# Pooled attention and a gated MLP: key rows in the order (key, pair), the first batch pooled on TensorE, new orders

## The chip, the cores and the metric

The kernel runs on one core of a Trainium2 chip. The core has TensorE (PE, matrix multiply), VectorE (DVE), ScalarE (ACT), GpSimd (POOL) and SyncE (SP, which here issues every DMA). The metric is device time in microseconds (us), the median of the runs shown; less is better.

## The reference, cut to what matters

```python
# q, k, v: (8 batches, 8 heads, 576 rows, 64), float32
k_p = k.reshape(B, H, 72, 8, D).mean(axis=3)      # keys and values are averaged over groups of 8 rows
v_p = v.reshape(B, H, 72, 8, D).mean(axis=3)
attn = softmax(q @ k_p^T / sqrt(D))               # 576 x 72 for each head
x = concat_heads(attn @ v_p)                      # (B, 576, 512)
h = relu(x @ w_in)                                # w_in 512 x 1024
u, v = h[..., :512], h[..., 512:]
v_n = (v - mean(v)) / sqrt(var(v) + 1e-6)
gated = u * (w_spatial @ v_n + b_spatial)         # w_spatial 576 x 576, over the rows of a batch
out = gated @ w_out                               # w_out 512 x 512
```

The weights w_in and w_out come as 64-bit floats, which the kernel takes apart into 32-bit halves.

## The kernel before

All eight batches run through one core, one after the other but overlapped. To keep float32 accuracy on TensorE's reduced-precision float32 format, most operands are split into a high and a low part, and a product is made of three matmuls (high by high, low by high, high by low).

The work of a batch is written as stages, each a Python generator whose `yield`s cut it into steps:

- `K` (`att_keys`): four DMAs (L289) bring the first 64 pooled groups of the keys of all heads into two staging tiles `st`, each 128 rows by 2 by 512 numbers (8 raw rows of 64 side by side); a fifth DMA (L276, `load_rest`) brings the other 8 groups into `st_r`. Then the 8 raw rows are added up: by DVE in three halvings (`pool_sum`, L257 and L262), or, where the stage's name ends in `^`, by TensorE in eight matmuls with the identity into one accumulator (`pool_pe`, L268), from where ACT copies them. The results are `kp` and `kr`.
- `KT` (`att_keys_t`): three transposes on TensorE (L312, L313), then four copies (L320, L321) into `kp_bd`, which holds the two heads of a pair block by block.
- `V` (`att_values`): the same for values (two DMAs at L335, one at L276), without transposes; results `vp` and `vr_s`. `W` splits them into high and low parts.
- `Q0` to `Q4` load 128 query rows each (64 in the last, L377) and transpose them (L382). `S0` to `S4` are scores (L394, into the one PSUM buffer `s_ps`) and softmax, `T` transposes the probabilities (L459, L461), `A` multiplies by the values (L477 to L480) and yields `xT`.
- `v`, `u`, `s`, `o` are the four matrix products of the MLP (L527 and L542, L568, L587 to L589, L610). `s` is followed by a product on DVE (L592), a high part on ACT (L598) and a low part on POOL (L601), which `o` reads.
- `wv`, `wu`, `wo`, `ws`, `wb` load and prepare blocks of the weights once. The 64-bit blocks cost ACT, DVE and POOL instructions each (L177 to L192); the low half comes either from POOL (L202, L204) or, with `^`, from three matmuls on TensorE (L196 to L198) and a copy on ACT (L200).

A `~` or `^` after a stage's name chooses such a variant. The order of everything is written out in three tables: `FIRST` for batch 0, `STEP` for batches 1 to 6, `LAST` for batch 7. Each word in them is one step of a stage; `-` and `+` move it to the batch before or after, capitals belong to the next batch. Instructions stand on each engine in exactly the order of that table, and every engine works strictly in its order. SP's queue of DMAs is one of them. Staging tiles of K, V, `ws` and `wo` share three buffers (tag "kv"), so a load waits until the tile that had its buffer has been read.

Quoted in short, what sets the shape of a key load before:

```python
keys = k[b].rearrange("(r a e) (s j) d -> r e a s (j d)", r=2, e=2, j=POOL)
nc.sync.dma_start(out=sts[r][:, e, :], in_=keys[r, e, :, :KM, :])
```

In DRAM one such DMA walks 2 pairs (a), in each 64 groups (s), in each 512 numbers that lie together (2 KB); in SBUF it fills 128 rows.

Of the kernel before, what the change touches and what calls it, by code (L numbers as in the profile page):

```python
# [8 lines left out]
F32 = mybir.dt.float32  # L9
# [14 lines left out]


FIRST = (
# [16 lines left out]
)  # L43
STEP = (
# [8 lines left out]
)  # L53
LAST = (
# [7 lines left out]
)  # L62


# [5 lines left out]
def pooled_attention_gmlp(ctx: ExitStack, tc: tile.TileContext, q, k, v, w_in, w_sp, b_sp, w_out, out):  # L70
    nc = tc.nc
    B, H, S, D = q.shape
    P = 128
# [196 lines left out]
    def ps_pool():  # L270
        return ps_big()[:, :(NG + 1) * D].rearrange("p (g d) -> p g d", d=D)
# [6 lines left out]

    def att_keys(t, b, alt=""):

        keys = k[b].rearrange("(r a e) (s j) d -> r e a s (j d)", r=2, e=2, j=POOL)
        kp = pl.tile([P, 2, 2, D], F32, name="kp", tag="kp")
        kr = pl.tile([2 * RR, 1, 2, D], F32, name="kr", tag="kr")
        acc = ps_pool() if "^" in alt else None
        sts = []
        for r in range(2):
            sts.append(pl.tile([P, 2, POOL * D], F32, name="st", tag="kv", bufs=3))
            for e in range(2):
                nc.sync.dma_start(out=sts[r][:, e, :], in_=keys[r, e, :, :KM, :])  # L289
            yield  # L290
        st = load_rest(k[b, :, KM * POOL:, :].rearrange("h (s j) d -> h s (j d)", j=POOL))
        yield
        for r in range(2):
            if acc is None:
                pool_sum(sts[r], kp[:, r])
            else:
                pool_pe(sts[r], acc[:, 2 * r:2 * r + 2, :])
            yield
        if acc is None:
            pool_sum(st, kr, nc.gpsimd if alt else nc.vector)  # L300
        else:
            pool_pe(st, acc[:2 * RR, NG:, :])
            yield
            nc.scalar.copy(kp.rearrange("p r e d -> p (r e) d"), acc[:, :NG, :])
            nc.scalar.copy(kr, acc[:2 * RR, NG:, :].unsqueeze(2).broadcast_to([2 * RR, 1, 2, D]))
        t["k"] = kp, kr

    def att_keys_t(kp, kr, alt=""):

        kt = ps_tr()  # L310
        for r in range(2):
            nc.tensor.transpose(out=kt[:, r * P:(r + 1) * P], in_=kp[:, r, :, :], identity=ident)  # L312
        nc.tensor.transpose(out=kt[:, 2 * P:2 * P + 2 * RR], in_=kr[:, 0, :, :], identity=ident[:2 * RR, :2 * RR])  # L313
        yield
        main = kt[:, :2 * P].rearrange("p (g s) -> p g s", g=NG)
        rest = kt[:, 2 * P:2 * P + 2 * RR].rearrange("p (g e s) -> p g e s", g=NG, e=2)
        for e in range(2):
            es = slice(e * D, (e + 1) * D)
            copy = nc.vector.tensor_copy if alt else nc.scalar.copy
            copy(kp_bd[es, :, e * SP:e * SP + KM], main[es])  # L320
            copy(kp_bd[es, :, e * SP + KM:(e + 1) * SP], rest[es, :, e, :])  # L321
            if e == 0:
                yield

    def att_values(t, b, alt=""):

        eng = nc.gpsimd if alt else nc.vector
        rows = v[b].rearrange("(g e) (s j) d -> g (e s) (j d)", e=2, j=POOL)
        vp = pl.tile([P, NG, D], F32, name="vp", tag="vp")
        vq = pl.tile([2 * RR, 1, D], F32, name="vq", tag="vq")  # L330
        acc = ps_pool() if "^" in alt else None
        sts, g2 = [], [slice(2 * r, 2 * r + 2) for r in range(2)]
        for r in range(2):
            sts.append(pl.tile([P, 2, POOL * D], F32, name="st", tag="kv", bufs=3))
            nc.sync.dma_start(out=sts[r], in_=rows[g2[r], :P].rearrange("g p f -> p g f"))  # L335
            yield
        st = load_rest(rows[:, P:])
        yield
        for r in range(2):
            if acc is None:  # L340
                pool_sum(sts[r], vp[:, g2[r], :], eng)
            else:
                pool_pe(sts[r], acc[:, g2[r], :])
            yield
        if acc is None:
            pool_sum(st, vq, eng)
        else:
            pool_pe(st, acc[:2 * RR, NG:, :])
            yield
            nc.scalar.copy(vp, acc[:, :NG, :])  # L350
            nc.scalar.copy(vq, acc[:2 * RR, NG:, :])
            yield
        vr_s = pl.tile([RR, NG, D], F32, name="vr_s", tag="vr_s")
        for r in range(2):
            rs = slice(r * RR, (r + 1) * RR)
            nc.vector.tensor_tensor(vr_s[:, 2 * r:2 * r + 2, :], vq[rs].broadcast_to([RR, 2, D]),
                                    mask[rs].unsqueeze(2).broadcast_to([RR, 2, D]), op=ALU.mult)
        t["v"] = vp, vr_s

    def att_values_split(vp, vr_s):  # L360
        for e in range(2):
# [328 lines left out]
```

## Time and profile before

| What | Value |
|---|---|
| runs | 618.44, 617.6, 617.88 us; median 617.88 |
| the profiled execution | 617.54 us |
| its span, first to last instruction | 615.7 us |
| TensorE busy | 573.3 us (93%) |
| VectorE, ScalarE, GpSimd busy | 346.1, 301.5, 266.6 us |
| mean granted TensorE clock | 0.989 |
| bytes moved by DMA | 46.15 MB, mean 75 GB/s |

The page's chain of work that ended last is TensorE for 88% of the span, with 4% on DMA and 3% on SP's queue:

```profile
PE 88%; DMA 4%; SPq 3%; ACT 2%; DVE 2%; issue 0%; DVEq 0%; ACTq 0%
```

"Busy" counts an engine's own work; "idle before" is the wait ahead of an instruction, and the name behind the arrow what ended it. An idle time matters only where the engine's next work is what the end of the kernel hangs on. Line numbers are those of the kernel before; in the changed kernel L289 is L290 and L335 is L337.

### The profile page before, as it was taken

What the parts mean: (1) busy time and instruction counts of PE and PEld (TensorE: products, weight loads), DVE (VectorE), ACT (ScalarE), POOL (GpSimd) and SP (SyncE); (2) the same over time, 40 slices, a digit from 0 to 9 for tenths busy, and PEclk for the clock granted to TensorE, in tenths of its full rate; (3) what the DMA queues carried; (4) which work ended last, traced back from release to release, by engine and by line L of the source; (5) the groups of instructions that cost most, each with busy time, mean ns of one, the idle gap of its engine ahead of it and who ended that gap; (6) DMA issues with size and microseconds to landing.
All of it is one profiled execution on the core that took longest, in us unless ns stands there. A gap on an engine that the chain in (4) does not pass through costs nothing.

```text
span 615.7 us, 9982 instructions
## 1 busy us (share of the span) xinstructions
PE 573.3 (93%) x3557; PEld 513.8 (83%) x3557; DVE 346.1 (56%) x809; ACT 301.5 (49%) x937; POOL 266.6 (43%) x394
## 2 busy tenths in 40 slices
PE   1177889999999999999999999999999999999997
PEld 0165779987899888998999888998999988998995
DVE  1389768973794676336664576346663665253320
ACT  1079648673665364164635374254634474353321
POOL 1024566486345643344524652354525562240430
PEclk9988989999999999999999999999999999999999
DMA  1694324333242131302221121303220000101002
GB/s 69 201 242 127 121 72 121 92 110 117 87 110 71 47 91 52 103 26 85 71 94 52 52 86 52 108 22 111 62 93 3 1 33 19 36 2 51 18 1 85
DMA packets 56433, 46.15 MB, mean 75 GB/s; under 512 B 38848, under 2 KB 40896, under 8 KB 56384
## 3 DMA queue, kind: packets, MB, share of 16 engines
q1 hardware_dynamic: 56384, 45.52, 24.5%
q8 instruction: 28, 0.46, 0.3%
q14 instruction: 21, 0.17, 0.1%
HBM read 36.08 MB, written 9.44 MB: 74 GB/s over the span
## 4 chain that ended last, share of the span: by engine, by line
PE 88%; DMA 4%; SPq 3%; ACT 2%; DVE 2%; issue 0%; DVEq 0%; ACTq 0%
PE mm L568 17%; PE mm L587 17%; PE mm L610 16%; PE mm L527 14%; PE s_ps L394 6%; PE tp L459 3%; PE mm L542 2%; PE tp L382 2%; DMA st<-in_k 2%; SPq L289 2%; DMA st_r<-in_k 2%; PE tp L477 1%; PE mm L589 1%; PE mm L588 1%; PE tp L480 1%; PE tp L478 1%
## 5 line engine op out<-in xcount | busy, mean ns | idle before, releaser
L568 PE MATMUL mm<-xT,win_h 128*128 128x320 f32 (+1 forms) x512 | 106.1, 300 | 0.0
L428 POOL TENSOR_TENSOR pm<-e,rs 128x576 f32<-128x576 f32 (+1 forms) x40 | 47.0, 1174 | 93.1 <-DVE rs L425 87.5
L568 PEld LDWEIGHTS mm<-xT,win_h 128*128 128x128 f32 x512 | 83.9, 190 | 1.8
L601 POOL TENSOR_TENSOR gT<-g,gT 128x256 fp32r<-128x256 f32 x64 | 47.5, 749 | 81.8 <-ACT gT L598 81.7
L527 PE MATMUL mm<-win_h,xT 128*128 128x512 f32 x256 | 82.0, 401 | 0.0
L610 PE MATMUL mm<-wout_h,gT 128*128 128x512 f32 x256 | 81.2, 398 | 0.0
L587 PE MATMUL mm<-wT_h,vn_h 128*128 128x256 f32 (+1 forms) x256 | 76.3, 298 | 0.0
L568 PE MATMUL mm<-xT,win_l 128*128 128x256 f32 (+1 forms) x256 | 75.9, 297 | 0.0
L587 PE MATMUL mm<-wT_h,vn_l 128*128 128x256 f32 (+1 forms) x256 | 75.6, 295 | 0.0
L587 PE MATMUL mm<-wT_l,vn_h 128*128 128x256 f32 (+1 forms) x256 | 75.4, 295 | 0.0
L592 DVE TENSOR_TENSOR g<-mm,ru 128x320 f32<-128x320 f32 (+1 forms) x64 | 28.4, 453 | 80.1 <-PE mm L589 75.1
L536 POOL TENSOR_TENSOR vn_l<-vv,vn_h 128x512 fp32r<-128x512 f32 x32 | 41.7, 1320 | 52.5 <-ACT vn_h L534 52.5
L610 PEld LDWEIGHTS mm<-wout_h,gT 128*128 128x128 f32 x256 | 47.2, 189 | 9.9
L527 PEld LDWEIGHTS mm<-win_h,xT 128*128 128x128 f32 x256 | 46.7, 188 | 10.0
L394 PE MATMUL s_ps<-kp_bd,qT 128*128 128x144 f32 (+1 forms) x320 | 49.7, 301 | 4.2 <-ACT e L420 2.8
L149 ACT ACTIVATE xT<-tp 128x256 fp32r<-128x256 f32 (+1 forms) x64 | 25.0, 414 | 58.1 <-PE tp L480 57.8
L527 PE MATMUL mm<-win_l,xT 128*128 128x512 f32 x128 | 50.7, 396 | 0.0
L610 PE MATMUL mm<-wout_l,gT 128*128 128x512 f32 x128 | 50.7, 396 | 0.0
L568 PEld LDWEIGHTS mm<-xT,win_l 128*128 128x128 f32 x256 | 48.7, 190 | 0.0
L394 PEld LDWEIGHTS s_ps<-kp_bd,qT 128*128 128x128 f32 (+1 forms) x320 | 43.2, 188 | 6.5 <-ACT e L420 3.5
L587 PEld LDWEIGHTS mm<-wT_h,vn_h 128*128 128x128 f32 x256 | 48.2, 188 | 0.4 <-DVE g L592 0.2
L587 PEld LDWEIGHTS mm<-wT_h,vn_l 128*128 128x128 f32 x256 | 48.2, 188 | 0.0
(146 smaller groups left out, 1311.9 us busy)
## 6 DMA issues: line engine op xcount, KB each, us to landing
st<-in_k SPq DMA_DIRECT2D x32, 256.0 KB
qt<-in_q SPq DMA_DIRECT2D x32, 256.0 KB
st<-in_v SPq DMA_DIRECT2D x16, 512.0 KB
out<-ob SPq DMA_DIRECT2D x32, 256.0 KB
stw<-in_moe_w_in SPq DMA_DIRECT2D x8, 512.0 KB
st<-in_moe_w_out SPq DMA_DIRECT2D x4, 512.0 KB
st<-in_moe_w_spatial SPq DMA_DIRECT2D x4, 288.0 KB
st_r<-in_k SPq DMA_DIRECT2D x8, 128.0 KB
```

What stands on the lines that cost most here:

```text
L149: nc.scalar.activation(hi, src, AF.Copy)
L289: nc.sync.dma_start(out=sts[r][:, e, :], in_=keys[r, e, :, :KM, :])
L394: nc.tensor.matmul(s_ps[:m, g // 2, (g % 2) * 2 * SP:(g % 2 + 1) * 2 * SP], lhsT=qT[:, g, :m], rhs=kp_bd[:, g, :], start=True, stop=True,)
L428: nc.gpsimd.tensor_tensor(pm[:m], em, rs[:m].unsqueeze(2).broadcast_to([m, H, SP]), op=ALU.mult)
L459: nc.tensor.transpose(out=tpv[:, g, :], in_=pm[:, g, :P], identity=ident[:m, :m])
L527: nc.tensor.matmul(a, lhsT=xT[:, i, o + c * P:o + (c + 1) * P], rhs=w[:, i, DH:], start=(i == 0 and j == 0), stop=(i == NK - 1 and j == 2))
L536: nc.gpsimd.tensor_tensor(t["vn_l"][:, c, :], vv, f32(t["vn_h"][:, c, :]), op=ALU.subtract)
L568: nc.tensor.matmul(a, lhsT=w[:, i, d * P:(d + 1) * P], rhs=xT[:, i, o + ts.start:o + ts.stop], start=(i == 0 and j == 0), stop=(i == NK - ...
L587: nc.tensor.matmul(a, lhsT=x[:, c, ds], rhs=y[:, c, ts], start=(c == 0 and j == 0), stop=False)
L592: nc.vector.tensor_tensor(g, a, t["ru"][:, d, ts], op=ALU.mult)
L601: nc.gpsimd.tensor_tensor(dst[:, d, 1, at:at + m], g[:, o:o + m], f32(dst[:, d, 0, at:at + m]), op=ALU.subtract)
L610: nc.tensor.matmul(a, lhsT=src[:, i, x, at:at + m], rhs=w[:, i, :], start=(i == 0 and j == 0), stop=(i == ND - 1 and j == 2))
```

## The change

Three things are changed at once. The key loads walk DRAM as 64 groups, in each 2 pairs, so that a row of SBUF is (key, pair) instead of (pair, key); the copies into `kp_bd` undo that order. In `FIRST` the stages K and V of batch 0 carry `^` and are pooled on TensorE. All three tables are new; the weight blocks with a low half on TensorE are five (wv0, wv3, wv1, wu1, wu2) instead of seven (wv1, wv3, wv2, wv0, wu2, wu0, wo3). The results `t["k"]` and `t["v"]` are named before the steps that fill them, so that a table may place the next stage's step earlier.

```diff
 FIRST = (
-    "wv1~^ wv1 wv1 -K wv1 -K wv3~^ -K -Q0 -V -K -K wv1 -K -Q0 wv3 -Q0 wv3 wv2^ -KT wv1 -KT -Q1 -V -V -KT -S0~ "
+    "ws2 ws2 -K^ ws2 wv0^ -K ws2 -K wv0 -K wv0 -K wv2 -K wv2 -K wv0 wv2 -KT wv2 -Q0~ -KT -Q0 -Q1 wv2 -V^ -Q0 "
...
 LAST = (
...
-    "s03 s00 s00 s11 s13 s02 s10 s12 s01 s01 s00 s03 s10 s03 s11 -o0 s12 s00 s02 s12 s12 s11 o1 o1 s11 o4 o2 "
-    "o3 o4 o2 o1 o3 o4 o0 o2 o3 o0 o0 "
+    "s01 s10 s03 s10 s11 s02 s11 s01 s10 s10 o0 o1 o1 -o3 s13 o1 s11 s13 s11 s13 s12 s13 o3 o3 o4 o3 o0 o0 o4 "
+    "o4 o2 o2 o2 "
...
     def att_keys(t, b, alt=""):
-        keys = k[b].rearrange("(r a e) (s j) d -> r e a s (j d)", r=2, e=2, j=POOL)
+        keys = k[b].rearrange("(r a e) (s j) d -> r e s a (j d)", r=2, e=2, j=POOL)
         kp = pl.tile([P, 2, 2, D], F32, name="kp", tag="kp")
         kr = pl.tile([2 * RR, 1, 2, D], F32, name="kr", tag="kr")
+        t["k"] = kp, kr
...
-                nc.sync.dma_start(out=sts[r][:, e, :], in_=keys[r, e, :, :KM, :])
+                nc.sync.dma_start(out=sts[r][:, e, :], in_=keys[r, e, :KM, :, :])
...
     def att_keys_t(kp, kr, alt=""):
-        main = kt[:, :2 * P].rearrange("p (g s) -> p g s", g=NG)
+        main = kt[:, :2 * P].rearrange("p (r s a) -> p r a s", r=2, a=2)
...
-            copy(kp_bd[es, :, e * SP:e * SP + KM], main[es])
+            copy(kp_bd[es, :, e * SP:e * SP + KM].rearrange("p (r a) s -> p r a s", r=2), main[es])
...
     def att_values(t, b, alt=""):
+        vr_s = pl.tile([RR, NG, D], F32, name="vr_s", tag="vr_s")
+        t["v"] = vp, vr_s
...
-        vr_s = pl.tile([RR, NG, D], F32, name="vr_s", tag="vr_s")
...
-        t["v"] = vp, vr_s
```

What this does to the engines' orders at the start. SP's queue of DMAs before, from its first (`stw` is a staged 64-bit weight block, `qt` a block of queries):

```order
L165 DMA stw<-in_moe_w_in 128x1024
L289 DMA st<-in_k 128x1x512 x4
L165 DMA stw<-in_moe_w_in 128x1024
L276 DMA st_r<-in_k 64x1x512
L377 DMA qt<-in_q 128x8x64
L335 DMA st<-in_v 128x2x512
```

and in the changed kernel:

```order
L237 DMA st<-in_moe_w_spatial 128x576
L290 DMA st<-in_k 128x1x512 x2
L165 DMA stw<-in_moe_w_in 128x1024
L290 DMA st<-in_k 128x1x512 x2
L276 DMA st_r<-in_k 64x1x512
L165 DMA stw<-in_moe_w_in 128x1024
L377 DMA qt<-in_q 128x8x64 x2
L337 DMA st<-in_v 128x2x512
```

A block of spatial weights now goes first, the four key loads are two and two around a weight block, and two query blocks stand ahead of the first value load.

TensorE's order before, from its first instruction (`x`, `z` and `win_h` belong to the low half of a weight block, `tp` and `mm` are PSUM tiles):

```order
L196 MATMUL mm<-x,ident 128x512
L197 MATMUL mm<-win_h,ident_m 128x512
L198 MATMUL mm<-z,ident_p 128x512
L382 MATMUL tp<-ident,qt 128x128 x4
L312 MATMUL tp<-ident,kp 128x128 x2
L313 MATMUL tp<-ident,kr 128x64
L394 MATMUL s_ps<-kp_bd,qT 128x144 x4
L382 MATMUL tp<-ident,qt 128x128 x4
```

and in the changed kernel:

```order
L242 MATMUL mm<-ident,st 128x128 x4
L244 MATMUL mm<-ident,st 64x128
L268 MATMUL mm<-st,ident 128x128 x16
L268 MATMUL mm<-st_r,ident 64x64 x8
L312 MATMUL tp<-ident,kp 128x128 x2
L313 MATMUL tp<-ident,kr 128x64
L382 MATMUL tp<-ident,qt 128x128 x4
L394 MATMUL s_ps<-kp_bd,qT 128x144 x4
L382 MATMUL tp<-ident,qt 128x128 x4
L268 MATMUL mm<-st,ident 128x128 x8
L394 MATMUL s_ps<-kp_bd,qT 128x144 x4
L268 MATMUL mm<-st,ident 128x128 x8
```

The 24 pooling matmuls of the keys stand ahead of the transposes of the pooled keys, those of the values between the first score groups; the first low half of a weight block has moved behind them.

DVE's order before, from the end of the setup (`m_100` and `mask` are constants made of the identity):

```order
L257 TENSOR_TENSOR st<-st 128x2x128
L137 TENSOR_TENSOR mask<-m_100 64x2
L262 TENSOR_TENSOR kp<-st 128x128
L257 TENSOR_TENSOR st<-st 128x2x256
L257 TENSOR_TENSOR st<-st 128x2x128
L262 TENSOR_TENSOR kp<-st 128x128
L257 TENSOR_TENSOR st_r<-st_r 64x256
L257 TENSOR_TENSOR st_r<-st_r 64x128
L262 TENSOR_TENSOR kr<-st_r 64x128
L182 TENSOR_SCALAR x<-x 128x512
```

and in the changed kernel:

```order
L137 TENSOR_TENSOR mask<-m_100 64x2
L151 TENSOR_TENSOR wT_l<-mm,wT_h 128x4x128
L182 TENSOR_SCALAR x<-x 128x512
L183 SCALAR_TENSOR_TENSOR x<-stw,x 128x512
L184 TENSOR_SCALAR y<-x 128x512
L182 TENSOR_SCALAR x<-x 128x512
L183 SCALAR_TENSOR_TENSOR x<-stw,x 128x512
L184 TENSOR_SCALAR y<-x 128x512
L385 COPY qT<-tp 128x512
```

The halvings of the key stages are gone from DVE's start; two weight blocks and the copy of the first query block stand there.

More of the change, by code (lines that the diff above doesn't have):

```diff
@@ L305, in att_keys @@
             nc.scalar.copy(kr, acc[:2 * RR, NG:, :].unsqueeze(2).broadcast_to([2 * RR, 1, 2, D]))
-        t["k"] = kp, kr
     def att_keys_t(kp, kr, alt=""):
```

56 rows, old and new, of tables (FIRST, LAST, STEP) are left out of this document.

## The prediction

> **What bounds the kernel now.** I read the page's first lines, then the busy time by stage, then the start in order of time, then the DMA engines in it.
>
> ```profile
> span 615.7 us, 9982 instructions
> PE 573.3 (93%) x3557; PEld 513.8 (83%) x3557; DVE 346.1 (56%) x809; ACT 301.5 (49%) x937; POOL 266.6 (43%) x394
> ```
>
> TensorE is idle for 42.4 us in all. The table by stage (start:end, length, then busy time and instructions of each engine, granted clock, DMA share, GB/s) says where:
>
> ```profile
> core 0: us, PE busy (x) PEld busy (x) DVE busy (x) ACT busy (x) POOL busy (x), PEclk, DMA share, GB/s
> 0.00:20.00 20.00, 3.24 (x4) 1.00 (x4) 4.29 (x14) 2.57 (x3) 2.72 (x10) 1.00 0.25 87
> 20.00:32.00 12.00, 1.84 (x7) 1.32 (x7) 4.72 (x11) 2.38 (x7) 0.00 (x0) 1.00 0.75 223
> 32.00:68.00 36.00, 27.23 (x133) 21.20 (x133) 30.21 (x73) 30.09 (x103) 15.78 (x21) 0.86 0.60 161
> 68.00:80.00 12.00, 8.93 (x50) 7.63 (x49) 10.07 (x20) 4.75 (x13) 5.28 (x8) 1.00 0.39 124
> 80.00:181.00 101.00, 101.00 (x641) 91.03 (x642) 73.95 (x165) 63.11 (x195) 58.26 (x75) 0.98 0.35 104
> 181.00:586.00 405.00, 405.00 (x2577) 368.69 (x2577) 219.68 (x523) 192.16 (x604) 177.71 (x270) 1.00 0.18 56
> ```
>
> From 80 us on TensorE never rests. What can be won is therefore before 80 us: 32 us in which every engine waits, then 36 us in which DVE and ACT are each 84% busy (30.21 and 30.09 of 36) and pace TensorE. The timeline's rows for that start (start, length, instruction, in brackets the idle time before it and its releaser):
>
> ```profile
> 1.18 11.22 SPq L289 DMA_DIRECT2D st<-in_k  x4
> 4.47 0.66 ACT L177 ACTIVATE x<-stw 128x512 f32<-128x512 f32 x1 [2.46 <-DMA stw<-in_moe_w_in]
> 15.80 0.69 DVE L257 TENSOR_TENSOR st<-st 128x512 f32<-128x512 f32 x1 [8.30 <-DMA st<-in_k]
> 26.54 1.15 DVE L257 TENSOR_TENSOR st<-st 128x512 f32<-128x512 f32 x2 [8.75 <-DMA st<-in_k]
> 27.66 0.66 ACT L177 ACTIVATE x<-stw 128x512 f32<-128x512 f32 x1 [20.68 <-DMA stw<-in_moe_w_in]
> 28.52 0.73 DVE L257 TENSOR_TENSOR st_r<-st_r 64x256 f32<-64x256 f32 x2 [0.50 <-DMA st_r<-in_k]
> 29.12 1.11 PE L382 MATMUL tp<-ident,qt 128*128 128x128 f32 x4 [11.02 <-DMA qt<-in_q]
> 32.20 2.29 PE L394 MATMUL s_ps<-kp_bd,qT 128*128 128x144 f32 x8 [1.24 <-ACT kp_bd L321]
> 67.95 0.74 PE L527 MATMUL mm<-win_h,xT 128*128 128x512 f32 x2
> 79.95 0.69 PE L312 MATMUL tp<-ident,kp 128*128 128x128 f32 x2 [3.07 <-DVE xT L485]
> ```
>
> All wait for loads. The first weight load, 512 KB issued at 0.7, is in use at 4.47. The two key stages, also 512 KB each, arrive at 15.80 and 26.54: 10.7 us apiece. Loads issued after them (weights, queries) land only when the keys have, at 27.66 and 29.12. The DMA view of 4.5 to 26.5 us, in 40 slices, tells why:
>
> ```profile
> DMA  0111111111111111111111113798797515599226
> GB/s 7 45 48 52 52 52 52 48 52 52 48 52 52 52 48 52 52 48 52 52 52 52 48 52 97 235 328 320 202 313 187 143 52 78 182 410 331 71 82 201
> ```
>
> While only keys move, the share is one tenth at 48 to 52 GB/s. Once the other loads flow it is 0.7 to 0.9 at 200 to 410. So the key load keeps about two of sixteen DMA engines busy (2/16 is 0.125), each at some 25 GB/s, and SP sits 11.22 us on four issues. The kernel's key load is the one whose outermost count in DRAM is 2 (the pair), beside 128 rows in SBUF; the loads of weights, values and queries run over 128 rows, or 64 and more, on both sides.
>
> **The change part by part.**
>
> *Keys in rows (key, pair).* The outermost count becomes 64; packets stay 2 KB. From below the gain is nothing, if the count is not the cause. From above it is the first weight load's pace: 512 KB in under 3.4 us, where a key stage takes 10.7. I take the upper end, because row length and SBUF side of the two loads are alike and the outer count is what differs. A rule of the Trainium skill speaks here: "DMA: Bandwidth & Descriptors", section "Why a DMA increments its semaphore by 16 and not by 1", says a copy runs on the largest number of engines up to 16 that divides the slowest dimension of both sides, so 2 before and 16 after. The share of one tenth agrees with its 2; by it the sum is that of the upper end, without it the lower end stays open.
>
> From batch 1 on the same keys load behind a TensorE that is 405 of 405 us busy, so SP's freed time is worth nothing there.
>
> *Start, to the first scores.* The queue of SP is rearranged: a block of the spatial weights first, then the first key stage, a weight block, the second stage, the rest of the keys, a weight block, and only then queries. Up to that block it is 2.4 MB; at 235 to 410 GB/s that is 6 to 10 us, and with the 2 to 3 us that the first load shows before data is in use, all is there by 9 to 13 us. TensorE becomes the pace of the start. Its prices, from timeline and chain:
>
> ```profile
> 40.99 1.06 PE L242 MATMUL mm<-ident,st 128*128 128x128 f32 x4
> 41.84 0.42 PE L244 MATMUL mm<-ident,st 128*64 128x128 f32 x1
> 30.02 0.63 PE L312 MATMUL tp<-ident,kp 128*128 128x128 f32 x2
> 31.24 0.36 ACT L320 COPY kp_bd<-tp 64x256 f32<-64x256 f32 x1
> 31.49 0.19 ACT L321 COPY kp_bd<-tp 64x32 f32<-64x32 f32 x1
> 83.66 0.86 PE mm L196 x2
> 84.52 0.23 PE mm L197
> 84.75 0.23 PE mm L198
> 84.99 0.98 PE s_ps L394 x8
> ```
>
> A pooling matmul (float32, 128x128 by 128 columns) has no row. Nearest is L394 with 144 columns: two records each, 0.29 us a record after idleness (2.29/8, at 32.20) and 0.12 in steady flow (0.98/8). So 8 matmuls of a key stage cost 2.0 to 4.6 us. The granted clock reads 1.00 at both places, so it does not explain the two. "TensorE: Matmul & The Clock Gate", Part 1 of the Trainium skill, has a half clock for about the first 3.4 us of activity; by it the first stage alone would cost 4.6 and all later ones 2.0, which moves the sum under 2 us.
>
> Step by step: spatial block in by 4.0; five transposes 1.5 (1.06 and 0.42) to 5.5; first stage cold, 4.6, to 10.1; second stage 2.5, near the warm end as it follows without a pause, to 12.6; the 8 matmuls of the rest, half as wide, 1.5, to 14.1. Then two copies on ACT 0.8 (by L320 and half of it), three transposes 0.8, four copies and a weight conversion between them 1.75 (twice 0.36 and 0.19, and 0.65), 0.3 for handing over: first scores at 17.7, say 17. With all matmuls warm it is 14, with all cold 20. Against 32.20 that is 15 us earlier, bounds 12 and 18. The interleaved copies from PSUM (L320) now step by two; I cost that at nothing, since even doubled it adds 0.7 us inside those bounds.
>
> *Scores to the first v matmul* (32.20 to 67.95, 35.75 us). DVE loses the value pooling of batch 0, which these rows give (busy time of L257, then of L262, in 31 to 39 us):
>
> ```profile
> 31.00:39.00 8.00, 2.90 (x6) 0.00 (x0) 1.00 0.79 207
> 31.00:39.00 8.00, 0.80 (x3) 0.00 (x0) 1.00 0.79 207
> ```
>
> That is 3.7 of its 30.21; ACT gains two copies, 0.6, and loses conversions that now stand before the scores (two L177 and two L180 there). TensorE gains 24 matmuls (16 of the key stages' kind and 8 half as wide: 5 us warm, 12 cold), on an engine 27.23 of 36 busy at its cold pace, with idle gaps of 9 us. So the stretch shrinks by 0 (ACT or TensorE takes over the pace) to 3.7; I take 33 us, nearer the DVE row, because TensorE's added work fits in its gaps. The first v matmul comes at 17+33 = 50, 18 us earlier.
>
> *Lower halves of weights on TensorE.* Seven before, five after; each is 1.32 us (0.86+0.23+0.23). One of the two saved lies behind the first v matmul: -1.3. The other lies in the paced stretch and counts nothing. POOL takes over two, 2.6 us each, hidden while it is 15.78 of 36 busy.
>
> *Order of the repeated batch.* Same instructions; the rest of the keys is pooled on DVE instead of POOL, 1 us per batch beside 185 idle us of DVE between 181 and 586. TensorE has no gap to lose there: nothing, with bounds of -2 and +9 (1.5 per batch) for new waits.
>
> *Last batch.* Now o3's matmuls stand right behind the last s; before, o1, which did not need it, stood between. The chain is
>
> ```profile
> L592 DVE TENSOR_TENSOR g<-mm,ru 128x320 f32<-128x320 f32 (+1 forms) x64 | 28.4, 453 | 80.1 <-PE mm L589 75.1
> L598 ACT ACTIVATE gT<-g 128x256 fp32r<-128x256 f32 x64 | 25.9, 418 | 26.4 <-DVE g L592 26.4
> L601 POOL TENSOR_TENSOR gT<-g,gT 128x256 fp32r<-128x256 f32 x64 | 47.5, 749 | 81.8 <-ACT gT L598 81.7
> ```
>
> 0.45+0.42+0.75, about 1.9 with handing over. Three quarters of o3 (2.1 us, 9 matmuls at 0.23) can run first. Bounds 0 and 1.9; I take 0.5.
>
> **Sum.** -18 -1.3 +0.5 = -18.8. The profiled execution took 617.54 around its span of 615.7, 0.34 under the median 617.88; the median becomes 599.
>
> **The rivals.**
>
> 1. *The paced stretch eats part.* Value pooling on TensorE stands in order before the second and third scores, and its second load waits until the first key stage is pooled. If they run cold and in the way, 5 to 8 of their 12 us are not hidden and the first v matmul comes at 55 to 58: 604 to 607. For it: TensorE was at its slow pace there; against: its gaps. 0.20.
> 2. *The key load stays slow* (the change does not do what it says). Then pooling on TensorE starts its last pieces at 26.5 and 28.5 as before, needs 2 to 4 us where DVE needed 1, so the first scores come 2 to 4 us later than before; less 0.8 for the other terms, and with 0 to 5 us of rival 1: 619 to 626. It decides if two key stages are still 10 us apart. 0.05.
> 3. *Better than the sum*: warm matmuls from the start and a stretch paced at over 90%: first scores at 14 to 15, first v at 44, 592. 0.10.
> 4. *The new repeated order waits*, 1 to 1.5 us in six batches: 605 to 608. For it: three orders are new at once; against: DVE, ACT and POOL are idle for about half of that stretch and can wait without being late. 0.07.
> 5. *Given back later*: DVE, 73.95 of 101 us busy from 80 to 181, cannot follow a TensorE that starts earlier, and takes all: 617.9, no change. Against: its work there is the same and moves along. 0.03.
>
> My sum has 0.55. Its own range is 594 to 604. With rivals 1 and 3 partly, the range is 590 to 609, leaving out 2 and 5, the ends of 1 and 3 and some of 4. Below 0.2% (1.2 us) this kernel's runs tell nothing apart. Faster: 0.55+0.20+0.10+0.07 = 0.92; same 0.03; slower 0.05.
>
> **What would show it.** Right: DMA share above 0.5 in the first 10 us; SP's key issues near 0.5 us each; first scores near 17, first v near 50; TensorE without gaps from about 62 us to the end; final stretch as before. Wrong: key stages 10 us apart; L268 rows in front of L394 rows that were ready; TensorE gaps after 70 us, above all in the repeated batches.

## The result, and the profile after

| | before | changed |
|---|---|---|
| median of four runs each, taken side by side | 618.16 us | 596.84 us |
| lowest to highest | 617.6 to 618.49 | 596.22 to 597.67 |
| ratio, 95% interval | | 0.9657, 0.964 to 0.9673 |
| the profiled execution / its span | 617.54 / 615.7 us | 597.35 / 595.5 us |

The changed kernel is 21.3 us faster by the medians, 20.2 by the two profiled spans. All figures of this document are of runs at a granted clock of 0.95 and more; one run of the experiment f3, 937.73 us at a granted clock of 0.559, is left out. The first lines of the changed kernel's page:

```profile
span 595.5 us, 10082 instructions
PE 579.5 (97%) x3645; PEld 520.9 (87%) x3645; DVE 348.3 (58%) x820; ACT 294.8 (49%) x903; POOL 260.3 (44%) x377
PE 92%; ACT 3%; DVE 2%; DMA 1%; issue 1%; SPq 0%; DVEq 0%; ACTq 0%
```

TensorE now has 88 instructions and 6.2 us of busy time more (579.5 against 573.3), and is idle for 16.0 us where it was idle for 42.4. The chain that ended last holds 1% DMA and no SP queue, where it held 4% and 3%. The table by stage, with the columns of the one in the prediction:

```profile
0.00:20.00 20.00, 12.98 (x61) 11.08 (x62) 5.64 (x15) 6.89 (x14) 6.36 (x13) 1.00 0.89 263
20.00:32.00 12.00, 11.81 (x90) 11.28 (x91) 8.27 (x19) 7.15 (x29) 4.09 (x6) 1.00 0.78 234
32.00:68.00 36.00, 30.86 (x168) 23.18 (x167) 31.57 (x76) 28.73 (x93) 18.47 (x27) 0.95 0.47 132
68.00:80.00 12.00, 12.00 (x70) 10.54 (x70) 9.03 (x22) 9.31 (x30) 9.94 (x12) 1.00 0.14 44
```

In the first 20 us the DMA engines are busy for 0.89 of the time instead of 0.25, and TensorE for 12.98 us instead of 3.24. From 68 us to its last matmul, 3.6 us before the end, it has no idle time. The start in order of time:

```profile
1.18 1.32 SPq L290 DMA_DIRECT2D st<-in_k  x2
3.18 1.19 SPq L290 DMA_DIRECT2D st<-in_k  x2
3.73 1.09 PE L242 MATMUL mm<-ident,st 128*128 128x128 f32 x4 [3.73 <-DMA st<-in_moe_w_spatial]
5.28 3.75 PE L268 MATMUL mm<-st,ident 128*128 128x128 f32 x16 [0.25 <-DMA st<-in_k]
10.74 3.75 PE L268 MATMUL mm<-st,ident 128*128 128x128 f32 x16 [1.71 <-DMA st<-in_k]
14.42 1.97 PE L268 MATMUL mm<-st_r,ident 64*64 64x64 f32 x16
19.75 2.26 PE L394 MATMUL s_ps<-kp_bd,qT 128*128 128x144 f32 x8 [0.88 <-DVE qT L385]
22.66 2.42 PE L268 MATMUL mm<-st,ident 128*128 128x128 f32 x16
53.09 0.73 PE L527 MATMUL mm<-win_h,xT 128*128 128x512 f32 x2
60.77 0.38 PE L312 MATMUL tp<-ident,kp 128*128 128x128 f32 x2
```

SP spends 2.5 us on four key loads instead of 11.22. The two key stages are in use at 5.28 and 10.74 (before: 15.80 and 26.54), the first scores stand at 19.75 (32.20), the first v matmul at 53.09 (67.95), and the key transposes of batch 1 at 60.77, without the wait of 3.07 us that they had.

Cut at the first v matmul, the time is told apart into busy and idle. TensorE before and, in the second fence, after:

```profile
0.00:67.95 67.95, 32.26 (x143) 23.47 (x143) 39.17 (x97) 34.99 (x111) 18.45 (x31) 0.92 0.53 150
67.95:615.70 547.75, 541.03 (x3415) 490.36 (x3414) 306.92 (x713) 266.48 (x828) 248.16 (x364) 1.00 0.21 66
```

```profile
0.00:53.09 53.09, 40.91 (x235) 33.43 (x235) 33.17 (x79) 33.47 (x108) 18.13 (x31) 0.97 0.64 190
53.09:595.50 542.41, 538.60 (x3412) 487.51 (x3411) 315.15 (x742) 261.29 (x796) 242.17 (x347) 1.00 0.23 66
```

Ahead of the mark 35.7 us of idle time became 12.2 and 32.26 us of work became 40.91: together -14.9. Behind it idle time fell from 6.7 to 3.8 and work by 2.4: together -5.3.

### The profile page after: what moved, and what is told of

It is laid out like the page before. It is cut to its first block, busy times and chain, and to the rows that moved or that the text cites. A ratio compares the mean times of both kernels' runs of the same rounds, so it can differ in the third digit from the quotient of the medians.

```text
span 595.5 us, 10082 instructions
## 1 busy us (share of the span) xinstructions
PE 579.5 (97%) x3645; PEld 520.9 (87%) x3645; DVE 348.3 (58%) x820; ACT 294.8 (49%) x903; POOL 260.3 (44%) x377
## 4 chain that ended last, share of the span: by engine, by line
PE 92%; ACT 3%; DVE 2%; DMA 1%; issue 1%; SPq 0%; DVEq 0%; ACTq 0%
PE mm L568 17%; PE mm L587 17%; PE mm L610 17%; PE mm L527 15%; PE s_ps L394 7%; PE tp L382 3%; PE tp L459 3%; PE mm L542 3%; PE mm L588 1%; PE mm L589 1%; PE tp L477 1%; PE mm L268 1%; PE tp L480 1%; PE tp L478 1%; PE tp L479 1%; DMA st<-in_k 1%
## 5 line engine op out<-in xcount | busy, mean ns | idle before, releaser
L568 PE MATMUL mm<-xT,win_h 128*128 128x320 f32 (+1 forms) x512 | 106.4, 300 | 0.2 <-DVE wT_l L251 0.2
L428 POOL TENSOR_TENSOR pm<-e,rs 128x576 f32<-128x576 f32 (+1 forms) x40 | 48.5, 1212 | 103.1 <-DVE rs L425 92.6
L568 PEld LDWEIGHTS mm<-xT,win_h 128*128 128x128 f32 x512 | 83.0, 188 | 3.6 <-issue 1.2
L610 PE MATMUL mm<-wout_h,gT 128*128 128x512 f32 x256 | 81.5, 399 | 0.0
L568 PE MATMUL mm<-xT,win_l 128*128 128x320 f32 (+1 forms) x256 | 75.6, 295 | 0.0
L592 DVE TENSOR_TENSOR g<-mm,ru 128x256 f32<-128x256 f32 (+1 forms) x64 | 28.3, 453 | 55.4 <-PE mm L589 37.7
L610 PEld LDWEIGHTS mm<-wout_h,gT 128*128 128x128 f32 x256 | 46.7, 188 | 9.8
L513 POOL TENSOR_TENSOR rstd<-rstd,neg_half 128x1 f32<-128x1 f32 (+1 forms) x40 | 22.7, 569 | 71.7 <-DVE rstd L511 71.6
L610 PE MATMUL mm<-wout_l,gT 128*128 128x512 f32 x128 | 50.6, 395 | 0.0
L401 DVE TENSOR_REDUCE mx<-s_ps 128x8 f32<-128x576 f32 (+1 forms) x40 | 30.1, 752 | 33.1 <-PE s_ps L394 32.0
L394 PE MATMUL s_ps<-kp_bd,qT 128*128 128x144 f32 (+1 forms) x320 | 48.2, 295 | 1.1 <-DVE qT L385 0.9
L149 ACT ACTIVATE pt_h<-tp 128x512 fp32r<-128x512 f32 (+1 forms) x40 | 22.6, 565 | 52.0 <-PE tp L459 50.9
```

What stands on the lines that cost most here:

```text
L149: nc.scalar.activation(hi, src, AF.Copy)
L394: nc.tensor.matmul(s_ps[:m, g // 2, (g % 2) * 2 * SP:(g % 2 + 1) * 2 * SP], lhsT=qT[:, g, :m], rhs=kp_bd[:, g, :], start=True, stop=True,)
L401: nc.vector.tensor_reduce(mx[:m], sv, axis=AX.X, op=ALU.max)
L428: nc.gpsimd.tensor_tensor(pm[:m], em, rs[:m].unsqueeze(2).broadcast_to([m, H, SP]), op=ALU.mult)
L513: nc.gpsimd.tensor_tensor(rstd[:m], rstd[:m], neg_half[:m], op=ALU.pow)
L568: nc.tensor.matmul(a, lhsT=w[:, i, d * P:(d + 1) * P], rhs=xT[:, i, o + ts.start:o + ts.stop], start=(i == 0 and j == 0), stop=(i == NK - ...
```

## The experiments

The theory: the gain comes from the key load, which ran on two DMA engines and now runs on all; TensorE pooling and the new orders add little. The main rival: the rows only shift work, and the gain comes from pooling on TensorE and the new orders. Lines of the changed kernel that do not stand below are unchanged; "old rows" is (pair, key), "new rows" is (key, pair).

**1. Taking the three parts apart**

Run e1: only the key rows are new; orders and pooling on DVE are those of before.

```diff
-        keys = k[b].rearrange("(r a e) (s j) d -> r e a s (j d)", r=2, e=2, j=POOL)
+        keys = k[b].rearrange("(r a e) (s j) d -> r e s a (j d)", r=2, e=2, j=POOL)
...
-            copy(kp_bd[es, :, e * SP:e * SP + KM], main[es])
+            copy(kp_bd[es, :, e * SP:e * SP + KM].rearrange("p (r a) s -> p r a s", r=2), main[es])
```

> Kernel before with the new key rows alone (old orders, key and value pooling of batch 0 on DVE). Load theory (the gain is the keys landing sooner, because the load is spread over all DMA engines): the two key stages are in use by about 5 and 9 us instead of 15.80 and 26.54, the first scores come near 17 instead of 32.20, the first v matmul near 51 instead of 67.95, and the 3.07 us gap of TensorE at 77 us, ahead of batch 1's key transposes, is gone or smaller: 597 to 603 us. Order theory (the old orders are paced by DVE and ACT anyway, and the new orders and TensorE pooling make most of the gain): 608 to 616 us.

Measured: 596.42 us (595.98 to 597.2), ratio 0.9656 [0.964, 0.9672]. That is the whole gain of the change, with one part of it. SP's and TensorE's rows at its start:

```profile
1.18 2.62 SPq L289 DMA_DIRECT2D st<-in_k  x4
14.87 2.29 PE L394 MATMUL s_ps<-kp_bd,qT 128*128 128x144 f32 x8 [1.24 <-ACT kp_bd L321]
```

and the time cut at its first v matmul:

```profile
0.00:47.54 47.54, 30.36 (x143) 20.42 (x144) 38.78 (x97) 34.71 (x111) 17.79 (x31) 0.96 0.75 218
47.54:594.20 546.66, 541.20 (x3415) 490.29 (x3414) 306.55 (x713) 266.45 (x828) 249.49 (x364) 1.00 0.22 65
```

Its first v comes at 47.54, 5.6 us earlier than in the changed kernel, which has 8.65 us more work on TensorE ahead of that mark than the kernel before; behind it the old orders take 546.66, 4.3 us longer than the new ones.

Run e2: the changed kernel with the old rows (the same edit the other way round).

> Changed kernel with the old key rows (pair, key); new orders and TensorE pooling stay. Load theory: DMA share near one tenth while keys move, key stages 10 us apart again, first scores at 33 to 36 us: 613 to 622 us, so at or above the kernel before. Order theory: 600 to 608 us.

Measured: 658.46 us (657.54 to 660.83), ratio 1.0665 [1.0639, 1.0691]: slower than the kernel before by 41 us, and some 40 above the expectation. What broke is not at the start, where the first v comes 1.2 us later than before (69.2), but in the repeated batches. The largest waits of TensorE, then SP's and ACT's (us in all, times, longest):

```profile
PE mm L568 <- ACT ob L614: 25.2, 4, 6.6
PE mm L268 <- DMA st<-in_k: 18.1, 2, 10.0
SPq L290 <- DMA st<-in_k: 65.4, 5, 13.4
ACT ob L614 <- DMA out<-ob: 44.3, 4, 12.4
```

SP's queue in one of these batches:

```profile
301.92 1.17 SPq L290 DMA_DIRECT2D st<-in_k  x2
317.54 1.06 SPq L290 DMA_DIRECT2D st<-in_k  x2
324.66 1.00 SPq L617 DMA_DIRECT2D out<-ob  x2
```

and, right behind it, the chain and TensorE's next row:

```profile
324.66 7.68 DMA out<-ob
332.45 0.59 ACT ob L614
```

```profile
333.09 0.90 PE L568 MATMUL mm<-xT,win_h 128*128 128x320 f32 x2 [6.29 <-ACT ob L614]
```

In the new repeated order the second pair of key loads follows the first on SP and has to wait until a staging tile has been loaded and read (13.4 us at most). That alone does no harm: the changed kernel, with the fast load, holds SP at this place nearly as long, 14.55 us for the four key loads where e2 needs 16.68,

```profile
265.49 14.55 SPq L290 DMA_DIRECT2D st<-in_k  x4
```

but there the stores are issued 1.6 us behind the key loads (281.60), and ACT waits for none of them. In e2 a query load (3.34 us) and the rest of the keys (2.43 us) hold SP for 6 us more behind the slow keys. Only then the stores go out, at 324.66; the one that ACT waits for lands 7.68 us later, at 332.34, ACT copies into the buffer that has come free, and TensorE's next u (L568) had waited for that copy. In the order of before the two pairs were not neighbours:

```profile
187.04 1.13 SPq L289 DMA_DIRECT2D st<-in_k  x2
211.21 1.10 SPq L289 DMA_DIRECT2D st<-in_k  x2
```

There 24 us lie between them, and SP waited for no key load in those batches. The new orders are made for a fast load and need it.

Run e3: K and V of batch 0 pooled on DVE, all else as changed.

```diff
-    "ws2 ws2 -K^ ws2 wv0^ ... wv2 -V^ -Q0 "
+    "ws2 ws2 -K ws2 wv0^ ... wv2 -V -Q0 "
```

> Changed kernel with batch 0's keys and values pooled on DVE, not TensorE; rows and orders new. If TensorE pooling was worth its place (it takes 3.7 us off the DVE work between scores and first v): first scores 2 to 3 us earlier, since DVE pools a stage in 1.4 us where TensorE took 3.75, but first v 0 to 3 us later than 53.09: 596 to 600 us. If TensorE pooling at the slow rate costs more than it frees: 591 to 595 us.

Measured: 598.2 us (596.92 to 599.2), 0.9682 [0.9661, 0.9704]. Pooling on TensorE is worth 1.4 us by the medians, in intervals that overlap; the first v stands at 52.7, as with it.

Run e4: old rows and pooling on DVE, so that the orders alone are new.

> Changed kernel with old key rows and DVE pooling: only the new orders are left of the change. Load theory: 612 to 620 us, within 1% of the kernel before. Order theory: 600 to 610 us.

Measured: 659.88 us (656.43 to 661.03), 1.0665 [1.0627, 1.0703]. As with e2, the orders fail without the fast load, whoever pools.

**2. Why the load is fast, and where it pays**

Run f1: the kernel before, rows (pair, key) kept, each key load cut into two DMAs of one pair, so that each walks 64 groups first.

```diff
-                nc.sync.dma_start(out=sts[r][:, e, :], in_=keys[r, e, :, :KM, :])
+                for a in range(2):
+                    nc.sync.dma_start(out=sts[r][a * KM:(a + 1) * KM, e, :], in_=keys[r, e, a, :KM, :])
```

> Kernel before, key rows still (pair, key), but each key load cut into two DMAs of one pair and 64 groups each, so that the outermost count in DRAM is 64 without any change of layout (eight issues instead of four). Engine theory (the outermost count of 2 keeps a load on two DMA engines): keys land as fast as with the new rows, first v matmul at 48 to 50 us, 596 to 600 us. Layout theory (it is the interleaving of the two pairs in the rows that makes the load fast): key stages 10 us apart as before, 613 to 619 us.

Measured: 597.21 us (596.97 to 597.93), 0.967 [0.9654, 0.9686], DMA engines busy 0.86 of the first 20 us at 257 GB/s:

```profile
0.00:20.00 20.00, 8.41 (x24) 5.58 (x25) 12.32 (x32) 7.01 (x14) 3.39 (x11) 1.00 0.86 257
```

Bytes, SBUF rows and copies are those of before, and there are twice as many DMAs; so what matters is the first count of the walk: 2 of it keep 0.1 of the engines busy, 64 nearly all. The pages' packet counts, of the kernel before, of e1 and of f1, say the same:

```profile
DMA packets 56433, 46.15 MB, mean 75 GB/s; under 512 B 38848, under 2 KB 40896, under 8 KB 56384
DMA packets 56881, 46.16 MB, mean 78 GB/s; under 512 B 39296, under 2 KB 41344, under 8 KB 56832
DMA packets 57393, 46.16 MB, mean 78 GB/s; under 512 B 39808, under 2 KB 41856, under 8 KB 57344
```

Packets of 512 B and more are as many in all three; the small ones are 448 more in e1 and 960 more in f1. One small packet for each engine that a key load uses would give just that: 32 loads on 16 engines instead of 2 are 32 x 14 = 448, and 64 loads on 16 instead of 32 on 2 are 64 x 16 - 32 x 2 = 960. (The next two runs, with 28 and 4 of the 32 loads changed, have 392 and 56 more: again 14 for each.) This is what the Trainium skill states in "DMA: Bandwidth & Descriptors", section "Why a DMA increments its semaphore by 16 and not by 1" (the largest number up to 16 that divides the slowest dimension of both sides), and these runs agree with it: DMA share 0.1 with 2 before, 0.86 with 64 here.

Runs f2 and f3: new rows in batches 1 to 7 only (f2), and in batch 0 only (f3), both from the kernel before; `fast` also chooses the copies.

```diff
+        fast = b > 0        # the other kernel: b == 0
-                nc.sync.dma_start(out=sts[r][:, e, :], in_=keys[r, e, :, :KM, :])
+                nc.sync.dma_start(out=sts[r][:, e, :], in_=keys[r, e, :KM, :, :] if fast else keys[r, e, :, :KM, :])
```

> Kernel before with the new rows in batches 1 to 7 only. If the gain lies in the first batch's start: first scores and first v as before (32 and 68 us), only the 3.07 us gap of TensorE ahead of batch 1's key transposes can go: 612 to 617 us. If the later key loads matter as much: below 608 us.

> Kernel before with the new rows in batch 0 only. If the gain lies in the start: first v near 47.5 us and 596 to 602 us, the upper end if batch 1's keys, again on two engines and now needed 20 us earlier, hold TensorE up before its key transposes. If the later key loads matter as much: above 606 us.

Measured: batches 1 to 7 alone 615.28 us (612.58 to 616.25, six runs), 0.9955 [0.9933, 0.9977]; batch 0 alone 601.85 us (600.62 to 601.91, three runs), 0.9743 [0.9721, 0.9766]; the kernel before beside them 617.41. So batch 0 alone carries 15.6 us and the others alone 2.1 (1.4 to 4.1 by the interval), but the two together, as in f1, 20.2: once batch 0 is early, the other batches' loads are worth 4.6. What the others can win stands in TensorE's waits from 60 us on, of the kernel before, of the first and of the second of these kernels:

```profile
PE tp L312 <- DVE xT L485: 3.1, 1, 3.1
```

```profile
PE tp L314 <- DVE xT L487: 1.0, 1, 1.0
```

```profile
PE tp L314 <- DVE xT L487: 3.8, 1, 3.8
```

It is the wait ahead of batch 1's key transposes (L312, here L314). The rows put it down to a DVE instruction, yet it shrinks with batch 1's keys and grows when only batch 0 is early (with both early it is 1.7 in e1 and 1.0 in f1). DVE's own rows, of the kernel before and of f3, show part of the way: DVE, in its order, stands before batch 1's second key stage until that load is in.

```profile
72.32 1.15 DVE L257 TENSOR_TENSOR st<-st 128x512 f32<-128x512 f32 x2 [0.97 <-DMA st<-in_k]
```

```profile
55.59 1.15 DVE L257 TENSOR_TENSOR st<-st 128x512 f32<-128x512 f32 x2 [1.95 <-DMA st<-in_k]
```

f2 and e1 have no such wait there. That f2's time and its wait both shrink by 2.1 us is chance, though: its profiled run is the fastest of its six (612.58) and has a span 4.9 us under that of the kernel before. 2.9 of these lie ahead of its first v (65.04 instead of 67.95), where its second scores took 1.25 us instead of 2.26, before any key load of batch 1 was issued; the rows of batches 1 to 7 can't be the reason of that part.

Run f5: the changed kernel with the keys at the head of SP's queue, K pooled on DVE, V on TensorE, and the spatial block later.

```diff
-    "ws2 ws2 -K^ ws2 wv0^ -K ws2 -K wv0 -K wv0 -K wv2 -K wv2 -K wv0 wv2 -KT wv2 -Q0~ -KT -Q0 -Q1 wv2 -V^ -Q0 "
-    "-KT wv3~^ wv2 -V wv0 -S0 ...
+    "-K -K -K -Q0~ wv0^ ws2 wv2 -K -K -Q0 -K -Q0 -KT -KT -KT wv0 -Q1 -V^ wv0 -S0 ws2 wv2 ws2 wv0 wv2 wv0 ws2 "
+    "wv3~^ wv2 -V wv2 wv2 ...
```

> Changed kernel with another start: the five key loads and one query block go first, batch 0's keys are pooled on DVE (idle then), its values still on TensorE, the block of spatial weights and the weight blocks come after. First scores at 11 to 14 us instead of 19.75. If the 33 us from there to the first v matmul stay: first v at 45 to 47 and 588 to 592 us. If that stretch is set by the work of DVE and ACT from the start of the kernel on, not from the first scores on: first v at 50 to 53 and 594 to 598 us.

Measured: 596.19 us (594.81 to 596.79), 0.9648 [0.9629, 0.9667], the same as the changed kernel within the intervals, and what the second reading said. The first scores come at 15.38 (later than the 11 to 14 expected) instead of 19.75, the first v at 52.5 instead of 53.09: 4.4 us won at the start, 0.6 left at the end of the stretch. Its DVE shows one place where they go:

```profile
16.04 0.43 DVE L182 TENSOR_SCALAR x<-x 128x512 uint32<-128x512 uint32 x1 [3.00 <-ACT x L177]
...
20.73 0.75 DVE L401 TENSOR_REDUCE mx<-s_ps 128x8 f32<-128x576 f32 x1
```

The scores end at about 17.7, but DVE, in the order written, converts weights first and takes their maximum at 20.73. Behind that the stretch has its own pace: in the changed kernel, from 30 to 50 us, DVE and ACT are busy for 18.36 and 18.61 of 20 us.

```profile
30.00:50.00 20.00, 15.66 (x84) 11.38 (x83) 18.36 (x44) 18.61 (x65) 6.64 (x10) 0.91 0.32 93
```

**3. Closing tests**

Run g1: the kernel of e1 (new rows, old orders) with batch 0's values pooled on TensorE.

```diff
-    ... -K -Q0 -V -K -K wv1 ... ws3 -S0 -S1 wv2 -V -V -S0 -Q2 ...
+    ... -K -Q0 -V^ -K -K wv1 ... ws3 -S0 -S1 wv2 -V -V -V -V -S0 -Q2 ...
```

> Old orders with the new key rows, and batch 0's values pooled on TensorE (keys stay on DVE). It takes 3.7 us of work off DVE between the first scores and the first v matmul. If DVE sets that stretch in the old order too: first v 2 to 4 us before the 47.5 of the rows alone, 592 to 595 us. If TensorE's pooling in the slow part costs as much as it frees: 595 to 599 us.

Measured: 602.34 us (600.78 to 603.63, five runs), 0.9742 [0.9723, 0.9762]. Both sides had missed: it costs 6 us, and the first v comes at 53.95 instead of 47.54. DVE is freed of 3.7 us of work and then waits (its longest wait from 14 to 33 us, then the stage from 20 us on):

```profile
DVE vr_s L356 <- ACT vq L351: 7.5, 1, 7.5
```

```profile
20.00:32.00 12.00, 10.37 (x75) 8.89 (x74) 4.86 (x13) 7.21 (x26) 2.27 (x4) 0.91 1.08 282
```

The pooled values come back through ACT (L351) only at 26.4, DVE stands at its next instruction in order (L356) for 7.5 us, and the softmax behind it is late: the third scores stand at 29.67 instead of 24.56. Moving work off the busiest engine made that engine wait for the work.

Run g2: the changed kernel with old rows and a third output buffer (also for the two other tiles of that tag, `y` and `t2`), which tests what e2's waits say.

```diff
-        ob = pl.tile([P, DO], F32, name="ob", tag="ob", bufs=2)
+        ob = pl.tile([P, DO], F32, name="ob", tag="ob", bufs=3)
```

> Changed kernel with the old rows (658.46 us) and a third output buffer. Reading of its trace: output stores issued behind the slow keys land 8 us late, both output buffers stay taken, ACT cannot copy out, TensorE waits 6 us at a time in u (L568). If that is it: most of the 25 us of TensorE's waits on ACT's output copy go, 625 to 640 us. If the wait only moves (to queries or values behind the same keys): 650 us or more.

Measured: 636.86 us (633.94 to 638.07), 1.0291 [1.0266, 1.0316]: 21.6 us of the 40 are back.

```profile
PE mm L568 <- ACT ob L614: 7.1, 2, 3.7
```

The wait for `ob` falls from 25.2 to 7.1 us, 18.1 less, so late stores were about half of what e2 lost (the third buffer of `y` and `t2` was not tried apart). What remains above the kernel before (18.5 us) is 4.5 us of idle time and 11.9 of longer busy time by the two pages (TensorE 585.2 busy of 632.1, before 573.3 of 615.7), and 2 that the profiled executions do not show. Of the 11.9, 6.2 are in the changed kernel too, whose TensorE has more to do.

Run g3: the new orders and TensorE pooling with old rows and one pair per DMA (the edit of f1).

> Changed kernel with the old rows, but each key load cut into two DMAs of one pair each (eight issues). If the new orders only need a fast key load, not the new rows: 596 to 600 us. If they depend on the rows in another way, or the four extra issues hold up SP's queue: above 603 us.

Measured: 596.15 us (595.37 to 600.16), 0.9652 [0.9624, 0.9681]. The changed kernel's time without its new rows, so the new orders need the fast load and nothing else of the layout. None of these kernels is faster than the changed one by more than the intervals.

## Why the prediction came out right, and where its steps did not

599.0 us was forecast and 596.84 measured. By steps:

- **The key load.** Right, and shown: two key stages 5.5 us apart instead of 10.7, DMA share 0.89 in the first 20 us, about 0.6 us for an issue of SP (0.5 forecast), and the count as the cause by f1. Rival 2 is out.
- **First scores at 17, bounds 14 to 20.** 19.75, so at the cold end. The mis-sized term is the second key stage, set at 2.5 us and starting at 10.1: it started at 10.74 after a wait of 1.71 for its load and took 3.75, as long as the first (set at 4.6). I had let it go near the fast rate because it should follow without a pause; a pause there was, and the slow rate outlasted it. The rest of the keys ended near 16.4 instead of 14.1. Another 0.7 was lost on paper: the steps added up to 17.7, and I went on with 17.
- **The stretch of 33 us to the first v.** 33.34. But the reason is only half shown: with DVE pooling (e3) the first v comes just as early, at 52.7, from first scores at 17.09. What the stretch gains by TensorE pooling, the key stages on TensorE lose ahead of it.
- **-18 at the first v.** -14.9 (53.09 against 67.95), by the term above.
- **-1.3 behind it.** -5.3. The step that failed is the sentence that SP's freed time is worth nothing from batch 1 on. I had quoted the wait of 3.07 us at 79.95 and put its disappearance into no term. The later keys are worth 2.1 us alone (f2) and 4.6 once batch 0 is early (f1 against f3). With the low half (1.3) the wait makes 4.4 of the 5.3. The remaining 0.9 fits what stood behind the wait: from 79.95 to 83.50, at a granted clock of 0.52, the key transposes and twelve records of u took 3.55 us, and the same in f2, behind a wait of 0.97, took 2.11 (76.48 to 78.59).
- **The repeated order, bounds -2 to +9.** No idle time of TensorE from 68 us to its last matmul: rival 4 did not come. That this is so only with the fast load (e2: +40) was in no step; my rival 2 would have been priced 619 to 626 where it costs 658.
- **The last batch, +0.5.** It came to nothing: TensorE waits for nothing there, and from its last matmul to the end both kernels take 3.6 us.
- **Rival 1** had a price of 604 to 607 for pooling that stands in the way. It did not come here; g1 shows a loss near that size in the old order (602 us), but by DVE waiting for the pooled values and not by TensorE's rate. **Rival 3** asked for first scores at 14 to 15 and a first v at 44; e1 has such scores (14.87) and f5 nearly (15.38), their first v come at 47.54 and 52.5, and both end at the same time as the changed kernel. **Rival 5** is out.

So two errors of opposite sign, 3 us too much at the start and 4.5 too little behind it, made a sum that was 1.4 off by the spans (18.8 against 20.2). The way that was forecast is right, a fast key load that brings the start forward; that the total came so close is luck. And two of the three parts of the change, pooling on TensorE and the new orders, added nothing that can be told apart from e1's key rows alone.

## What to carry to other kernels

Look at the outermost count of a load in DRAM before its order in the queue: here that one count was worth all of the 21 us, and two DMAs of one pair each did as well as a new layout. An order written for fast loads is a contract: with the slow load the new order cost 40 us more than the old one, about half of it through output stores that stood behind slow loads in SP's queue. And before work is moved to an idle engine, ask where its result comes back and who stands in order behind it; the move cost 6 us in one order (g1) and was worth nothing that can be told apart in the other (e3).

## What the runs showed of the hardware beyond that

TensorE ran at its slow rate for far longer than its first few us. In the changed kernel it works from 3.73 on with no pause over 1.71 us, and still the stage at 10.74 takes 3.75 us for 16 records, the scores at 19.75 2.26 us for 8, and the pooling at 22.66 2.42; the next such 16 take less:

```profile
24.92 1.15 PE L394 MATMUL s_ps<-kp_bd,qT 128*128 128x144 f32 x8
25.90 1.95 PE L268 MATMUL mm<-st,ident 128*128 128x128 f32 x16
```

The granted clock of these stretches reads 1.00. "TensorE: Matmul & The Clock Gate", Part 1 of the Trainium skill, has a half clock for about 3.4 us of sustained activity; the change of rate by a factor of two agrees, its time does not show at this start: the longest stretch without a pause, 10.74 to 16.39, was slow throughout, and the fast rate came some 19 us after the first matmul (in g3 some 12 us). What the short pauses do to that time, no run here shows alone. The fast rate is lost again after a wait: in e2, two L568 records take 0.90 us behind the wait of 6.29, and 0.46 ahead of it. There the granted clock shows it, at 0.50 for the first 3.6 us:

```profile
324.77 0.46 PE L568 MATMUL mm<-xT,win_h 128*128 128x320 f32 x2
```

```profile
333.09:336.70 3.61, 3.61 (x13) 3.61 (x14) 0.57 (x2) 1.35 (x5) 1.30 (x1) 0.50 0.21 77
```

In the kernel before, the scores at 38.94 are as slow as the first ones at 32.20 (2.26 and 2.29 us), at granted clocks of 0.52 and 1.00; so at the start a reading of 1.00 does not tell the slow rate from the fast one, and the slow rate behind a wait goes with half the clock. A gap costs its own length and the slow matmuls behind it. TensorE's busy time in e2 is 592.3 us where the same instructions take 579.5 in the changed kernel. Of these 12.8 us an estimate puts about 9 down to that: behind the wait at 333.09 twelve records of L568 take 3.57 us and the next twelve of L610 3.16, in steady flow 1.76 and 2.80, so 2.2 us for each of the four waits. The rest was not traced.
